# Attention over clusters with two MLPs on one core: a second product in unsplit float32, cluster dots in four column groups, and a new set of priorities

## The chip, the cores and the metric

The kernel runs on one core of one Trainium2 chip, as one program. The metric is the device time of one execution in microseconds; of several executions the median is given.

## The reference

For 2 batches of 8 heads, 768 tokens and a head width of 64, every query and key is assigned to one of 16 centroids of its head, and a query sees the keys of its own cluster only. The heads' outputs, put side by side as 1536 tokens of width 512, go through two MLPs.

```python
q_assign = np.argmax(np.einsum('bhsd,hcd->bhsc', q_n, c_n), axis=-1)
k_assign = np.argmax(np.einsum('bhsd,hcd->bhsc', k_n, c_n), axis=-1)
mask = q_assign[:, :, :, None] == k_assign[:, :, None, :]
scores = np.where(mask, scale * np.matmul(q, k.transpose(0, 1, 3, 2)), -1e9)
attn = softmax(scores); x = np.matmul(attn, v)
h = np.maximum(x @ w_in, 0.0)
y = h * h @ w_out
out = (1.0 / (1.0 + np.exp(-(y @ w_gate))) * (y @ w_val)) @ w_out2
```

Here `softmax` stands for the lines that subtract the maximum, exponentiate and divide by the sum. The weights of the MLPs come as 64-bit words and are turned into float32 on the chip.

## The kernel before, in words

**Attention.** There are 96 score tiles, 6 to each of 16 heads, of 128 queries by 768 keys. A tile `s` is made on TensorE (`t_qk`), its row maximum on VectorE (`t_max`, line 978), its exponential on ScalarE (`t_exp`, line 993). Then most tiles are split into two halves of 16 bits, the high one by ScalarE (line 330) and the low one by VectorE (`t_lo`, line 1018, which frees the score bank), transposed by a DMA, and multiplied with the values on TensorE (`po`). Twelve pairs of tiles (`by_pe`) stay in float32 and are transposed by TensorE instead (`t_turn_pe`, line 1055, tiles `tb` and `ptf`). A few tiles (`by_pool`) are split by GpSimd.

**Cluster assignment.** For every four heads the products of queries and keys with the centroids (`CB`) are made in two halves (`half_dots`, line 671) in a bank `ah`. Rows of tokens are the stationary operand there, so that tokens come out on partitions: twelve matmuls of 32 columns to a half. `half_most`, `half_reach` on VectorE, `half_turn` on TensorE, `half_keep`, `half_count` and `half_first` then find the first largest centroid. The first two heads are assigned ahead of all others by `pair_dots` (line 445) with the operands the other way round: four matmuls of 384 columns, each into 32 partitions of its own (tile `as`). Seven half-groups go by `half_dots`. The tiles `T` and `M` are the operands of the scores, built from the raw queries and keys and the assignment.

**MLPs.** Tokens are taken in three chunks of 512. Nearly every product is made of float32 operands cut into two parts that TensorE takes at full rate (type fp32r): high by high, high by low and low by high, so three matmuls. Weights are loaded as words, turned into float32 (`magnitude` to `lower`, tiles `wi0m`, `wo0m` and so on) and split by `split_tasks` (line 1391, `wo0h` and `wo0l`); the first MLP's hidden tiles are squared into the bank and split by `split_bank` (line 1423, `g_..h` and `g_..l`). Of the first MLP (`g1` and `g2`, products `g` and `y`) chunk 0 is worked off by itself, in four groups of four hidden tiles; its tokens are complete after the first batch. Chunks 1 and 2 follow, and then the second MLP (`pg`, `pv`, `o`).

**The order of the work.** A planner (class `Planner`) walks through time once, when the program is built. Each piece of work has the engines on which it can run with an estimated cost, a priority, the buffers that it takes and gives back, and sometimes a gate on how far ahead it may run. Of the pieces that are ready, an engine takes the one with the lowest priority number, and that fixes the order of every engine's instructions. The numbers of `PLAN` (line 32) set the priorities, the gates and what an engine's time is worth. Where the planner sees a hole on TensorE during attention, `fill` (line 617) puts matmuls there whose results are not used:

```python
n = min(8, int((gap - 700) // 250))
```

All plain matmuls stand on line 323, ScalarE's copies on line 330, VectorE's on 332 and GpSimd's on 334.

Of the kernel before, what the change touches and what calls it, by code (L numbers as in the profile page):

```python
# [32 lines left out]
    "asg_p": -2000, "assign": 15, "assign_step": 2.0, "base": 70, "build": 4, "build2": 6.4,  # L33
    "clamp_p": -1700, "conv": 8, "conv_gate": 14, "d": 3.8, "dup_a": 1700, "dup_p": 900,
    "dup_q": 200, "e_bufs": 2, "exp": 1.6, "g_gate": 3, "g_split": -7.9, "group": 4, "h_gate": 11,
    "h_split": 2.1, "hi": 3.9, "hi_a": -1000, "hi_p": 99999, "hip_p": 600, "hip_v": 400,
    "keep_x_v": 1700, "lead": 0, "lead2": 7, "lead_min": 10, "lead_slope": 0, "lo": -0.2,
    "lo_v": 600, "load_gate": 8, "margin": 5, "max": 1, "oh_p": 900, "pe_keep": -1.9,
    "pe_keep_v": 300, "pe_turn": 1.6, "pv": -1.7, "pv_pe": 5.1, "qk": 2.0, "qk_hi_a": -200,
    "qk_hi_p": 2500, "qk_lo_v": -100, "qk_sc_p": -400, "raw": 30, "relu": 1.7, "s_hi_a": -500,  # L40
    "s_hi_p": 1800, "s_lo_v": -1400, "spare": 0, "split_gate": 8, "square_v": 900, "third": 1,
    "turn": 13.3, "v_hi_a": 1200, "v_hi_p": 1300, "v_later": 100000, "v_lo_v": 700, "v_split": 19,
    "v_stat": 11, "w_hi_a": -900, "w_hi_p": -100, "w_lo_v": -800, "w_load": 8.2, "w_mag_v": 3100,
    "w_split": 3.0, "wait_a": 0.2, "wait_p": 1.0, "wait_q": 0, "wait_t": 0, "wait_v": 0,
    "worth_a": 600, "worth_p": 0, "worth_v": 1200, "x": -1.3, "x0": 109, "x1": 226, "x_gate": 5,
    "x_split": 3.4, "y_gate": 12, "y_keep": 7.1, "y_keep_v": 500, "y_split": -4.3,
    "by_pe": (1, 4, 7, 10, 13, 16, 19, 21, 23, 26, 30, 33,),
    "by_pool": (3, 14, 53, 71, 72,),
# [6 lines left out]
class Task:  # L55


    __slots__ = ("fn", "on", "prio", "waits", "users", "left", "ready", "take", "give", "gate", "end", "price", "port")

    def __init__(self, fn, on, prio, after, take, give, gate, kind, port):  # L60
        self.fn, self.on, self.prio = fn, on, prio

        self.port = port
# [21 lines left out]
class Planner:  # L85


    def __init__(self, start):
        self.free = dict(start)
        self.units = {}  # L90
        self.avail = []
        self.freeing = []
        self.count = 0
        self.total = 0
        self.port = 0.0
        self.fill = None

    def add(self, fn, on, prio, after=(), take=(), give=(), gate=None, at=0.0, kind="", port="vp"):
        t = Task(fn, on, prio, after, take, give, gate, kind, port)
        t.ready = max(t.ready, at)  # L100
        self.total += 1
        if not t.left:
            self.avail.append(t)
        return t

    def start(self, t, e, now):
        for res, n in t.take:
            self.units[res] -= n
        if e == "t" and self.fill is not None:
# [20 lines left out]

    def can(self, t, e, now):
# [6 lines left out]
        if t.gate is not None and not t.gate():  # L138
# [4 lines left out]
    def soon(self, best, e, now):  # L143
# [7 lines left out]
            and (u.gate is None or u.gate())  # L151
# [36 lines left out]
def kernel(  # L188
# [77 lines left out]
    def provide(name, pool, tag, n):  # L266
        places.setdefault(name, []).append([pool, tag, [0] * n])
        units[name] = units.get(name, 0) + n
# [1572 lines left out]
```

## Time and profile before

| what | value |
|---|---|
| median of 3 runs | 824.47 us (823.18 to 824.98) |
| span of the profiled execution | 821.0 us |
| busy: TensorE, VectorE, ScalarE, GpSimd | 783.9, 551.2, 456.1, 236.4 us |
| mean granted clock of TensorE | 0.977 |
| data moved by DMA | 96.85 MB |

The profile gives the span of one execution, from its first to its last instruction. Its own whole time is not recorded apart; the runs' times hold the span and what lies around it, and the median is 3.5 us above the span. In the rows PE is TensorE's matmuls, PEld its weight loads, DVE VectorE, ACT ScalarE, POOL GpSimd. PEclk is the clock that TensorE was granted as a share of full speed. An arrow with a name behind a row's idle time says which instruction ended the wait. A float32 matmul appears as two records.

### The profile page before, as it was taken

The numbers are of one execution on the slowest core, as the hardware profiler recorded it, in microseconds if no ns is written. First come the engines' busy times: TensorE is split into PE (matmuls) and PEld (weight loads), VectorE is DVE, ScalarE is ACT, GpSimd is POOL, SyncE is SP. The second block draws the span as 40 slices with busy tenths as digits, with TensorE's granted clock in tenths as the row PEclk, the third lists the DMA queues.
The fourth block names the chain that finished last, engine by engine and source line by source line (L and its number), as shares of the span: only waits on it lengthen the run. The fifth ranks groups of instructions, "written<-read, shape, count | busy, mean of one in ns | idle before, by whom it ended". The sixth has DMA issues, their size and how long they took to land.

```text
span 821.0 us, 12751 instructions
## 1 busy us (share of the span) xinstructions
PE 783.9 (95%) x4869; PEld 657.1 (80%) x4869; DVE 551.2 (67%) x885; ACT 456.1 (56%) x822; POOL 236.4 (29%) x304
## 2 busy tenths in 40 slices
PE   7898988999998989899999999999999999999998
PEld 4687978897887867688888888888888888888886
DVE  7889788879999997968375868844334437960300
ACT  8768779869887775578483654422222225630300
POOL 7755434845564222303030322200010004200000
PEclk9989899989999999999999999999999999999999
DMA  7777887758798998424131323312111213100101
GB/s 246 139 155 166 169 171 207 146 110 174 168 197 151 213 208 267 142 94 151 52 129 58 126 74 103 128 52 97 58 51 55 100 51 107 48 26 26 40 26 39
DMA packets 133742, 96.85 MB, mean 118 GB/s; under 512 B 114800, under 2 KB 114992, under 8 KB 133680
## 3 DMA queue, kind: packets, MB, share of 16 engines
q1 hardware_dynamic: 133680, 96.03, 46.1%
q8 instruction: 38, 0.62, 0.3%
q14 instruction: 24, 0.20, 0.1%
HBM read 62.10 MB, written 3.15 MB: 79 GB/s over the span
## 4 chain that ended last, share of the span: by engine, by line
PE 59%; ACT 0%; issue 0%
PE y L323 12%; PE o L323 12%; PE pv L323 12%; PE pg L323 12%; PE g L323 11%; PE xq L1245 0%; ACT ot L1631 0%
## 5 line engine op out<-in xcount | busy, mean ns | idle before, releaser
L323 PE MATMUL s<-M,T 128*128 128x384 f32 x360 | 87.9, 374 | 15.0 <-DVE hl L1018 10.5
L978 DVE TENSOR_REDUCE nm<-s 128x1 f32<-128x768 f32 x96 | 89.9, 949 | 12.4 <-PE s L323 12.0
L1602 DVE SCALAR_TENSOR_TENSOR gv<-th,pv 128x512 f32<-128x512 f32 x36 | 24.6, 687 | 87.7 <-PE pv L323 86.3
L323 PEld LDWEIGHTS s<-M,T 128*128 128x128 f32 x360 | 64.2, 202 | 23.2 <-DVE hl L1018 9.5
L1595 ACT ACTIVATE th<-pg 128x512 f32<-128x512 f32 x36 | 21.5, 598 | 109.9 <-PE pg L323 109.9
L993 ACT ACTIVATE s<-s,nm 128x768 f32<-128x768 f32 x70 | 61.2, 874 | 22.6 <-DVE nm L978 22.3
L1018 DVE TENSOR_TENSOR hl<-s,hl 128x768 f16<-128x768 f32 x70 | 65.9, 946 | 7.8 <-ACT hl L330 7.6
L330 ACT ACTIVATE hl<-s 128x768 f16<-128x768 f32 x70 | 56.4, 814 | 0.5
L1631 ACT ACTIVATE ot<-o 128x512 f32<-128x512 f32 x12 | 7.2, 598 | 79.4 <-PE o L323 79.4
L323 PEld LDWEIGHTS <-pt 128*128 128x128 f16 x1296 | 43.1, 101 | 9.1 <-issue 6.5
L1339 POOL TENSOR_SCALAR wgm<-wgm 128x512 f32<-128x512 f32 x12 | 8.6, 719 | 141.1 <-ACT wgm L1331 125.9
L323 PE MATMUL po<-vh,pt 128*128 128x64 f16 x864 | 47.0, 197 | 1.9 <-DMA pt<-hl 1.2
L323 PE MATMUL po<-vl,pt 128*128 128x64 f16 x432 | 44.2, 197 | 0.0
L323 PEld LDWEIGHTS po<-vr,ptf 128*128 128x128 f32 x288 | 38.2, 208 | 0.9 <-DVE xp L1110 0.8
L323 PE MATMUL po<-vr,ptf 128*128 128x64 f32 x288 | 37.9, 288 | 0.0
L1571 DVE TENSOR_TENSOR yf<-yf,y 128x512 f32<-128x512 f32 x36 | 24.6, 684 | 16.3 <-PE y L323 15.8
L1529 ACT ACTIVATE r<-g 128x512 f32<-128x512 f32 x48 | 28.7, 597 | 11.3 <-PE g L323 10.6
L1339 POOL TENSOR_SCALAR wi1m<-wi1m 128x512 f32<-128x512 f32 x16 | 10.1, 633 | 76.3 <-ACT wi1m L1331 64.9
L915 POOL TENSOR_TENSOR T<-raw,T 64x768 fp32r<-64x768 f32 x14 | 26.6, 1898 | 17.8 <-ACT T L330 9.1
L1535 ACT ACTIVATE g<-r 128x512 f32<-128x512 f32 x48 | 29.0, 604 | 1.1
L921 POOL TENSOR_TENSOR M<-raw,M 64x768 fp32r<-64x768 f32 x15 | 28.1, 1871 | 1.0
L993 ACT ACTIVATE e<-s,nm 128x768 f32<-128x768 f32 x26 | 23.5, 905 | 7.6 <-DVE nm L978 7.2
(605 smaller groups left out, 2390.8 us busy)
## 6 DMA issues: line engine op xcount, KB each, us to landing
wi0r<-in_moe_w_in_dram SPq DMA_DIRECT2D x16, 512.0 KB, 4.0
wo0r<-in_moe_w_out_dram SPq DMA_DIRECT2D x16, 512.0 KB, 4.7
wi1r<-in_moe_w_in_dram SPq DMA_DIRECT2D x16, 512.0 KB, 3.3
wo1r<-in_moe_w_out_dram SPq DMA_DIRECT2D x16, 512.0 KB, 3.3
wgr<-in_moe_w_gate_dram SPq DMA_DIRECT2D x12, 512.0 KB, 3.3
wvr<-in_moe_w_val_dram SPq DMA_DIRECT2D x12, 512.0 KB, 3.3
w2r<-in_moe_w_out_dram SPq DMA_DIRECT2D x12, 512.0 KB, 3.3
raw<-in_q_dram SPq DMA_DIRECT2D x8, 384.0 KB, 4.7
```

The lines of the kernel that those rows point to most:

```text
L323: nc.tensor.matmul(o, lhsT=l, rhs=r, start=a, stop=z)
L330: nc.scalar.activation(out=out, in_=in_, func=AF.Copy, scale=scale)
L915: eng(e).tensor_tensor(out=T1[j][q], in0=raw[k][r], in1=T1[j][r].bitcast(F32), op=ALU.subtract)
L921: eng(e).tensor_tensor(out=M2[j][r], in0=raw[k][r], in1=M1[j][r].bitcast(F32), op=ALU.subtract)
L978: nc.vector.tensor_reduce(out=NM[n], in_=sc_ps[n][:, :, :HS], axis=AX.XY, op=ALU.max, negate=True)
L993: nc.scalar.activation(out=y, in_=x, func=AF.Exp, bias=NM[n], accum_out=SM[n // NQ][:, i : i + 1],)
L1018: nc.vector.tensor_tensor(out=halves(hl[:, n % 2, 1]), in0=x[:, :, :HS], in1=halves(hl[:, n % 2, 0]), op=ALU.subtract,)
L1529: nc.scalar.activation(out=r, in_=banks["g1", c, f], func=AF.Relu)
L1535: nc.scalar.activation(out=p, in_=r, func=AF.Square)
L1571: nc.vector.tensor_tensor(out=yf[c, dm], in0=yf[c, dm], in1=p, op=ALU.add)
L1595: nc.scalar.activation(out=t, in_=p, func=AF.Tanh, scale=0.5)
L1602: nc.vector.scalar_tensor_tensor(out=o, in0=t, scalar=1.0, in1=p, op0=ALU.add, op1=ALU.mult)
```

## The change

It does three things. For 12 of the 16 hidden tiles of chunk 0 (groups 0, 1 and 3, named by `whole`) the second product of the first MLP takes the weights and the squared activations unsplit, in float32, one matmul in place of three. The dots of `half_dots` have their operands exchanged: four matmuls of 384 columns, each into 32 partitions; a copy (`half_out`) and three transposes (`half_flip`) then bring tokens onto partitions. And nearly all numbers of `PLAN` are others, `by_pe` and `by_pool` among them. Besides, the planner's estimates of these pieces are set to the new form, the score operands are given back by every tile of a head instead of the last, and gates and pools are counted where a piece is planned instead of by closures.

```diff
 PLAN = {
-    "asg_p": -2000, "assign": 15, "assign_step": 2.0, "base": 70, "build": 4, "build2": 6.4,
+    "asg_p": -3875, "assign": 14.0, "assign_step": -3.1, "base": 80, "build": 4.0, "build2": 6.3,
...
-    "by_pe": (1, 4, 7, 10, 13, 16, 19, 21, 23, 26, 30, 33,),
-    "by_pool": (3, 14, 53, 71, 72,),
+    "by_pe": (1, 4, 7, 10, 13, 16, 19, 23, 26, 33, 35, 45),
+    "by_pool": (41, 44, 56, 81, 86, 93),
+    "nudge": {},
+    "whole": (0, 1, 3),
...
+        for s in range(2):
+            for y in range(2):
+                pl, h0 = (y, hf) if gp > 0 else (-gp, y)
+                r0 = s * 64 + y * 32
+                mm(
+                    a[r0 : r0 + 32, :HS], CB[:, 2 * gr + pl].rearrange("p j c -> p (j c)"),
+                    raw[s, b, 2 * gr + pl][:, h0 * HS : (h0 + 1) * HS], True, True,
+                )
+        AX_[gp, hf] = a
+
+    def half_out(e, gp, hf):
+        if hf == 0:
+            AX_[gp, "d"] = at.tile([P, S], F32, tag="d", name=f"d{gp % (NG + 1)}")
+        copy(e, AX_[gp, "d"][:, hf * HS : (hf + 1) * HS], AX_[gp, hf][:, :HS])
+
+    def half_flip(gp, hf):
         for x in range(3):
-            for s in range(2):
-                for y in range(2):
-                    pl, t = (y, 3 * hf + x) if gp > 0 else (-gp, 3 * y + x)
-                    c0 = x * P + s * 64 + y * 32
-                    mm(
-                        a[:, c0 : c0 + 32], raw[s, b, 2 * gr + pl][:, t * P : (t + 1) * P],
-                        CB[:, 2 * gr + pl].rearrange("p j c -> p (j c)"), True, True,
-                    )
-        AX_[gp, hf] = a
+            nc.tensor.transpose(
+                AX_[gp, hf][:, x * P : (x + 1) * P],
+                AX_[gp, "d"][:, hf * HS + x * P : hf * HS + (x + 1) * P], ident,
+            )
...
-                dots, {"t": 2400}, pr, after=last + [x for k in keys for x in raw_after(*k)],
+                dots, {"t": 680}, pr, after=last + [x for k in keys for x in raw_after(*k)],
...
+            t = add(
+                lambda e, gp=gp, hf=hf: half_out(e, gp, hf), {"a": 400, "v": 465}, pr + st_,
+                kind="ptk", after=[t], port="",
+            )
+            t = add(lambda e, gp=gp, hf=hf: half_flip(gp, hf), {"t": 330}, pr + st_, after=[t])
...
+            if f in self.whole:
+                self.split[f, uses[0]] = [self.conv[f]]
+                return
...
+    WHOLE = [f for f in range(NF1) if f // gsize(0) in PLAN["whole"]]
+    W2 = [Weights(w_out, f"wo{c}", False, w2[c], () if c else WHOLE) for c in range(2)]
...
+        if c == 0 and f in WHOLE:
+            h = slab(F32, f"h{c}_{f}")
+            hT[c, f] = [h]
+            if e == "a":
+                nc.scalar.activation(out=h, in_=r, func=AF.Square)
+            else:
+                nc.vector.tensor_tensor(out=h, in0=r, in1=p, op=ALU.mult)
+            drop(p)
+            drop(r)
+            return
...
+        if c == 0 and f0 in WHOLE:
+            ops = [(W.m[f][:, ds_], hT[c, f][0]) for f in range(f0, f0 + gs)]
```

What it moves is seen in the order of the instructions. On PE, the dots of one half of heads 4 to 7 of the first batch (`ah` is their bank, `raw` the queries and keys, `eq` and `tw` the later steps, `po` the product with the values); first before, then with the change:

```order
L323 MATMUL ah_1_220_832<-CB,raw_0_2_12_137 128x32
L323 MATMUL ah_1_220_832<-CB,raw_0_3_50_313 128x32
L323 MATMUL ah_1_220_832<-CB,raw_0_2_13_139 128x32
L323 MATMUL ah_1_220_832<-CB,raw_0_3_56_322 128x32
...
L323 MATMUL ah_1_220_832<-ident_150,eq_1_888 128x128
...
L323 MATMUL ah_1_220_832<-tw_1_933,before 128x384
```

```order
L344 MATMUL ah_1_189_747<-raw_0_2_12_137,CB 32x384
L344 MATMUL ah_1_189_747<-raw_0_3_50_314,CB 32x384
L344 MATMUL ah_1_189_747<-raw_0_2_13_139,CB 32x384
L344 MATMUL ah_1_189_747<-raw_0_3_78_389,CB 32x384
L344 MATMUL po_184_734<-vr_0_4_121,ptf_160_641 128x64
...
L713 MATMUL ah_1_189_747<-ident,d_540 128x128 x3
L344 MATMUL s_198_776<-M_0_109,T_0_105 128x384 x2
```

Before, the first four rows come three times. Now they come once, and behind six matmuls of another tile follow the transposes, which read `d`, ScalarE's copy of the dots; the next score tile is queued behind them.

On PE, the first output tile `y` of group 0 of chunk 0 (`g_0h`, `g_0l` the split squares, `h_0` the unsplit one, `wo0h`, `wo0l`, `wo0m` the weights); before and with the change:

```order
L323 MATMUL y_0_0_878_2938<-g_0h_2641,wo0h_462_1653 128x512
L323 MATMUL y_0_0_878_2938<-g_0l_2648,wo0h_462_1653 128x512
L323 MATMUL y_0_0_878_2938<-g_0h_2641,wo0l_466_1664 128x512
L323 MATMUL y_0_0_878_2938<-g_1h_2730,wo0h_741_2548 128x512
L323 MATMUL y_0_0_878_2938<-g_1l_2741,wo0h_741_2548 128x512
L323 MATMUL y_0_0_878_2938<-g_1h_2730,wo0l_785_2668 128x512
```

```order
L344 MATMUL y_0_0_812_2754<-h_0_735_2479,wo0m_396_1410 128x512
L344 MATMUL y_0_0_812_2754<-h_1_768_2612,wo0m_600_2071 128x512
L344 MATMUL y_0_0_812_2754<-h_2_802_2709,wo0m_716_2407 128x512
L344 MATMUL y_0_0_812_2754<-h_3_805_2711,wo0m_775_2642 128x512
L344 MATMUL s_822_2773<-M_0_109,T_0_105 128x384 x2
```

Twelve matmuls to an output tile have become four, and a score tile stands right behind them.

On ACT, the hidden tiles 0 and 1 of chunk 0 (`r` the rectified tile, `ptf` and `hl` copies for attention, `e` and `s` exponentials, `sm` and `nm` their sums and maxima); before and with the change:

```order
L1529 ACTIVATE r_0_760_2589<-g_0_0_724_2469 128x512
L330 ACTIVATE ptf_758_2583<-tb_0_759_2584 128x512
L1535 ACTIVATE g_0_0_724_2469<-r_0_760_2589 128x512
L993 ACTIVATE e_770_2621,sm_746_2560<-s_755_2575,nm_763_2595 128x768
L1529 ACTIVATE r_1_778_2650<-g_0_1_744_2554 128x512
L330 ACTIVATE wo0h_779_2653<-wo0m_594_2059 128x512
...
L1535 ACTIVATE g_0_1_744_2554<-r_1_778_2650 128x512
L330 ACTIVATE wo0h_806_2721<-wo0m_787_2670 128x512
L330 ACTIVATE g_1h_2730<-g_0_1_744_2554 128x512
```

```order
L351 ACTIVATE d_2448<-ah_0_720_2419 128x384
L1565 ACTIVATE r_0_733_2456<-g_0_0_725_2428 128x512
L1574 ACTIVATE h_0_735_2479<-r_0_733_2456 128x512
L351 ACTIVATE T_1_106<-raw_1_1_299_1103 64x768
L351 ACTIVATE tw_0_2524<-ah_0_720_2419 128x384
L351 ACTIVATE M_1_110<-raw_1_1_358_1291 64x768
...
L1565 ACTIVATE r_1_763_2585<-g_0_1_743_2519 128x512
L1574 ACTIVATE h_1_768_2612<-r_1_763_2585 128x512
```

The squares go straight into `h`, the conversions to high parts (`wo0h`, `g_1h`) are gone from between them, and copies of `T`, `M` and `d` stand among them.

## Rows read from the trace of the kernel before

**Rows 1.** The page's summary of engines, and TensorE's clock in 40 slices.

```profile
PE 783.9 (95%) x4869; PEld 657.1 (80%) x4869; DVE 551.2 (67%) x885; ACT 456.1 (56%) x822; POOL 236.4 (29%) x304
...
PEclk9989899989999999999999999999999999999999
```

**Rows 2.** Windows by stage: length, busy time of each engine (instructions), clock, DMA share, GB/s.

```profile
0.00:24.00 24.00, 18.98 (x64) 11.63 (x65) 16.46 (x43) 18.10 (x33) 15.55 (x40) 0.93 0.69 223
24.00:138.00 114.00, 102.45 (x1084) 92.39 (x1083) 99.94 (x153) 91.06 (x177) 58.31 (x76) 0.94 0.79 170
138.00:301.00 163.00, 151.24 (x1376) 130.64 (x1375) 147.62 (x230) 133.37 (x241) 84.63 (x95) 0.95 0.84 168
301.00:337.00 36.00, 30.97 (x239) 25.22 (x238) 30.46 (x52) 22.21 (x42) 8.72 (x12) 0.97 0.82 241
337.00:821.00 484.00, 480.25 (x2112) 397.19 (x2110) 256.69 (x411) 191.38 (x333) 69.14 (x82) 1.00 0.22 74
```

**Rows 3.** The chain that ended last, in order of time: start us, us, what.

```profile
336.22 0.66 PE xq L1245 x4
336.87 12.54 PE y L323 x48
...
390.21 21.76 PE y L323 x96
...
719.33 97.93 PE o L323 x432
```

**Rows 4.** Waits of PE over the whole span: us in total, times, longest us.

```profile
PE s L323 <- DVE hl L1018: 11.1, 15, 2.2
...
PE s L323 <- ACT e L993: 2.4, 3, 1.1
...
PE ah L323 <- ACT tw L330: 1.2, 2, 0.6
```

**Rows 5.** PE's groups by form; its timeline from 6.2 us; line 323 from 6.9 us.

```profile
L1055 PE MATMUL tb<-ident,e 128*128 128x128 f32 x144 | 23.6, 288 | 4.2 <-ACT ptf L330 2.7 <-DVE ot L717 1.1 <-DVE sc L585 0.3
...
L323 PE MATMUL ah<-CB,raw 128*128 128x32 f32 x168 | 21.0, 285 | 0.0
...
L323 PE MATMUL fill<-ident 128*128 128x512 f16 x20 | 5.3, 380 | 0.5 <-DVE xp L1110 0.4
...
6.20 0.85 PE L323 MATMUL as<-raw,CB 128*32 128x384 f32 x8 [0.55 <-DVE CB L438]
...
L323 PE MATMUL busy<-raw,ident x14: 486/486/590, 7.0 to 11.3; 128*128 128x384 f32 x14
```

**Rows 6.** Windows around three dips of PE's clock; columns as in rows 2.

```profile
48.00:53.00 5.00, 5.00 (x44) 5.00 (x43) 4.92 (x8) 3.04 (x7) 2.12 (x3) 1.00 0.85 157
53.00:61.00 8.00, 7.46 (x49) 6.64 (x48) 6.38 (x9) 3.91 (x7) 3.56 (x5) 0.57 0.85 199
162.00:166.00 4.00, 3.38 (x32) 3.05 (x30) 2.87 (x5) 4.00 (x9) 3.76 (x4) 1.00 0.00 0
166.00:173.00 7.00, 7.00 (x32) 7.00 (x32) 4.31 (x7) 1.37 (x3) 2.03 (x3) 0.51 0.61 112
247.00:251.00 4.00, 2.33 (x10) 1.13 (x8) 4.00 (x8) 2.82 (x6) 0.12 (x1) 1.00 1.08 108
251.00:255.00 4.00, 3.38 (x40) 3.07 (x40) 4.00 (x7) 3.88 (x7) 0.51 (x1) 0.57 0.52 152
```

**Rows 7.** Groups by form on ACT and DVE: busy us, mean ns, idle before.

```profile
L330 ACT ACTIVATE T<-raw 64x768 fp32r<-64x768 f32 x13 | 10.9, 840 | 2.2 <-PE s L323 2.1
...
L330 ACT ACTIVATE wo0h<-wo0m 128x512 fp32r<-128x512 f32 x14 | 8.9, 632 | 1.6 <-DVE wo0m L1360 1.5
...
L1404 DVE TENSOR_TENSOR wo0l<-wo0m,wo0h 128x512 fp32r<-128x512 f32 x8 | 8.4, 1054 | 0.0
...
L1404 DVE TENSOR_TENSOR wi0l<-wi0m,wi0h 128x512 fp32r<-128x512 f32 x10 | 7.4, 737 | 1.0 <-ACT wi0h L330 0.7
...
L332 DVE TENSOR_SCALAR T<-T 64x768 fp32r<-64x768 f32 x7 | 5.2, 743 | 0.1
```

More of the change, by code (lines that the diff above doesn't have):

```diff
@@ L39 @@
[L39 to L44, printed above, removed]
@@ L55, with __init__ @@
 class Task:
-    __slots__ = ("fn", "on", "prio", "waits", "users", "left", "ready", "take", "give", "gate", "end", "price", "port")
-    def __init__(self, fn, on, prio, after, take, give, gate, kind, port):
+    __slots__ = ("fn", "on", "prio", "waits", "users", "left", "ready", "take", "give", "gate", "end", "price", "port", "place", "gain")
+    def __init__(self, fn, on, prio, after, take, give, gate, kind, port, place, gain):
         self.fn, self.on, self.prio = fn, on, prio
-        self.port = port
+        self.port, self.place, self.gain = port, place, gain
         self.price = {
@@ L95, in __init__, with add @@
         self.port = 0.0
+        self.place = 0
         self.fill = None
-    def add(self, fn, on, prio, after=(), take=(), give=(), gate=None, at=0.0, kind="", port="vp"):
-        t = Task(fn, on, prio, after, take, give, gate, kind, port)
+    def add(
+        self, fn, on, prio, after=(), take=(), give=(), gate=None, at=0.0, kind="", port="vp", place=None, gain=()
+    ):
+        prio += PLAN["nudge"].get(self.total, 0)
+        t = Task(fn, on, prio, after, take, give, gate, kind, port, place, gain)
         t.ready = max(t.ready, at)
@@ L108, in start @@
             self.units[res] -= n
+        for res, n in t.gain:
+            self.units[res] = self.units.get(res, 0) + n
+        if t.place is not None:
+            self.place = t.place
         if e == "t" and self.fill is not None:
@@ L129, in start, with open @@
                 self.avail.append(u)
+    def open(self, k, ahead, n):
+        if k > self.place + ahead:
+            return False
+        if not n:
+            return True
+        x = self.units["xn"]
+        return k <= self.place + 1 and x == 0 or self.units["S"] >= n + PLAN["spare"] + x
     def can(self, t, e, now):
@@ L137, in can @@
             return False
-        if t.gate is not None and not t.gate():
+        if t.gate is not None and not self.open(*t.gate):
             return False
@@ L150, in soon @@
             and all(self.units[r] >= n for r, n in u.take)
-            and (u.gate is None or u.gate())
+            and (u.gate is None or self.open(*u.gate))
             for u in self.avail
@@ L972, in t_qk @@
         sc_ps[n] = s
-        if n == NQ - 1:
+        if n < NQ and thold[0].readers == 0:
             drop(TM)
@@ L1290 @@
     at_ = {u: k for k, u in enumerate(order)}
-    pos = [0]
     BASE = PLAN["base"]
     def near(k, ahead):
-        return lambda: k <= pos[0] + ahead
-    def spare(k, n):
-        return k <= pos[0] + 1 and units["xn"] == 0 or units["S"] >= n + SPARE + units["xn"]
+        return (k, ahead, 0)
     def pr_of(k, early):
@@ L1372, in tasks @@
             )
-            def room():
-                return k <= pos[0] + CONVGATE and spare(k, 1)
+            room = (k, CONVGATE, 1)
             t = add(
@@ L1660 @@
                 t = add(
-                    started(k, lambda e, c=c, f=f, k=k, part=part: g1_part("g1", c, f, part, k)),
-                    {"t": 907}, pr, after=after, take=[("m", 1)] if part == 0 else [], give=give,
+                    lambda e, c=c, f=f, k=k, part=part: g1_part("g1", c, f, part, k),
+                    {"t": 907}, pr, place=k, after=after, take=[("m", 1)] if part == 0 else [], give=give,
                 )
@@ L1668 @@
             )
+            if c == 0 and f in WHOLE:
+                t = add(
+                    lambda e, c=c, f=f: square(e, c, f), {"a": 520, "v": 600}, pr - PLAN["h_split"], kind="square",
+                    after=[t], take=[("S", 1)], give=[hold("r", 1, 1), bh], port="",
+                )
+                hsplit[c, f] = [t]
+                continue
             t = add(
@@ L1689 @@
                 t = add(
-                    started(k, lambda e, c=c, g=g, dm=dm, part=part: g2_part(c, g, dm, part)),
-                    {"t": 113 * 3 * gs}, pr, after=after, take=[("m", 1)] if part == 0 else [],
+                    lambda e, c=c, g=g, dm=dm, part=part: g2_part(c, g, dm, part),
+                    {"t": 113 * 3 * gs if nx == 2 else 429 * gs}, pr, place=k, after=after, take=[("m", 1)] if part == 0 else [],
                     give=give if part else [],
@@ L1744 @@
                 t = add(
-                    started(k, lambda e, c=c, t=t_, part=part: g4_unit(e, c, t, part)),
-                    {"t": 2040}, pr, after=after,
+                    lambda e, c=c, t=t_, part=part: g4_unit(e, c, t, part),
+                    {"t": 2040}, pr, place=k, after=after,
                     take=[("m", 1)] if part == 0 else [],
```

87 lines of the change are left out of this document (47 added, 40 removed).

## The prediction

> **What bounds the kernel now.** I read the page's summary first: TensorE (PE) is busy for 783.9 of 821.0 us, 95%, and its clock row shows dips in the first 17 of 40 slices and almost none later [rows 1]. The windows by stage say where the other 37 us are [rows 2]. From 337 us on PE is busy for 480.25 of 484 us at full clock. The idle time lies ahead of that: 5.0 us in the start (0 to 24), 11.6 us in stage 1 (24 to 138, the score tiles of the first batch, with no other matmul work to fill in), 11.8 us in stage 2 (138 to 301, second batch, filled up with tokens 0 to 511 of the first MLP) and 5.0 us in stage 3 (301 to 337, what trails the last score tile). The chain that ended last confirms it: from 336.22 us it is PE alone, piece behind piece, to the end [rows 3]. So the whole time is PE's work plus the holes in the first 337 us. Cheaper work on another engine helps only where it closes a hole, and work added to PE costs its full length wherever it stands.
>
> The holes: PE's waits name VectorE (DVE) first, 11.1 us until the subtraction that frees a score bank; ScalarE (ACT) is behind 2.4 us of the same kind [rows 4]. DVE is busy for 147.62 of 163 us in stage 2, ACT for 133.37, PE for 151.24 [rows 2]: three engines near full, DVE with the least room to catch up. Besides holes there is a slower clock. The granted clock is 0.94 in stage 1 and 0.95 in stage 2 [rows 2], worth 6.8 and 8.2 us of work at full clock. It falls towards 1.2 GHz right behind the dots of 48 to 53 us, in which PE was busy the whole time with short matmuls, behind those of 162 to 166 us, and behind idle time as at 247 to 251 us [rows 6].
>
> **The change, part by part.** The profiled execution has a span of 821.0 us; the median of the runs is 824.47, 3.5 us more, which I add at the end.
>
> Dots. Seven half-groups of twelve 32-column matmuls take 21.0 us, 3.00 us each [rows 5]. Now each is four matmuls of 384 columns in four column groups, which the start of this kernel already does once: 0.85 us for the four, with the next matmul starting no later than they end. To this come three f32 transposes, 23.6 us / 144 = 0.164 us each, 0.49 us [rows 5]. 1.34 instead of 3.00 us, seven times: **-11.6 us** on PE. At the other end, four in a row at 0.66 us each (next paragraph but one) and 0.49 would be 3.14 us: +1.0 us in all. The row of the same shape decides for the first.
>
> The copy between dots and transposes is a new wait: the transpose stands on PE ahead of the next score tile, and the copy stands on ACT among exponentials. The nearest rows are PE's waits for an ACT copy of the same bank, 1.2 us in 2 of 7 cases, and for an exponential, at most 1.1 us [rows 4]. Bounds 0 and 7 x 1.1 = 7.7 us; I take the former's **+1.2 us**, since it is the same bank and engine.
>
> Second product. 48 f32 matmuls of 512 columns replace 144 at 21.76 / 96 = 0.227 us [rows 3]. The f32 price: `busy` is 7 matmuls of 384 columns, recorded as 14 halves that start from 7.0 to 11.3 us, so 0.662 us each, or 0.684 with the last one's 0.486 us counted in [rows 5]; for 512 columns 0.882 to 0.912. Against 3 x 0.227 = 0.680 this costs 48 x 0.202 = **+9.7 us**, at most +11.1. It is on PE, so nothing hides it.
>
> Fill matmuls fall from 20 to 14: 6 x 5.3 / 20 us [rows 5] = **-1.6 us**. PE's own sum is -11.6 + 1.2 + 9.7 - 1.6 = -2.3 us.
>
> The other engines. The unsplit product needs no high and low parts of 12 weight tiles and 12 activations. With the new priorities DVE loses 5 weight subtractions (1.054), 12 of activations (priced as the weight subtraction at 0.737) and 20 copies of T and M (0.743) [rows 7]: 29.0 us; in all, 63 fewer DVE instructions precede its last score maximum, 425 to 362, 15 of them in the first 48 tiles and 48 in the rest. ACT loses 21 high parts (0.632) but takes 12 copies of T and M (0.840) [rows 7] and the 7 new copies (under 0.632, being shorter): 346 to 351 instructions ahead of its last exponential. But they shift: 154 to 175 up to the 48th tile, 192 to 176 after it. None of this shortens the time by itself; it is worth what idle time it takes away.
>
> Stage 1: PE has four half-groups less to do (-6.6 us), but ACT has 21 more instructions. I let the stage shorten by half of PE's relief: **+3 us** idle. Bounds: -4 (a third of the 11.6 us goes) and +17.4 (rival 3). Stage 2: DVE's instructions there fall by a fifth (229 to 181) and ACT's by a twelfth, so of the 11.8 us I take half, **-6**; bounds 0 and -11.8. What is late next there is PE itself. Stage 3: 132 f32r matmuls and 16 f32 ones now stand behind the last score tile, where 144 f32r stood (44 instead of 33 us), so more work covers the trailing transfers: **-2**, bounds 0 and -5.0. They are work moved, not added.
>
> Clock: the spell behind the dots lost (1 - 0.57) x 8 = 3.4 us [rows 6]; that behind the dots of 162 to 166 us lost (1 - 0.51) x 7 = 3.4 us too. Full-width streaming in place of the short matmuls should spare one of the two: **-3.4**; bounds +3.4 (a new spell behind a hole in stage 1) and -10.
>
> Sum: -2.3 + 3 - 6 - 2 - 3.4 = -10.7; 821.0 - 10.7 = 810.3, and with 3.5 us **813.8 us**.
>
> **Rivals.**
> 1. Only PE's own sum counts; holes and clock stay: 821.0 - 2.3 + 3.5 = 822.2 us. For it: the chain from maximum to exponential to subtraction keeps its length per tile. Against: DVE stands behind the largest wait.
> 2. The relief is taken whole: half of stage 2's and 3's idle (-8.4), stage 1's unchanged, the clock's loss cut by three spells of 3.4 us (-10.2): 803.6 us. For it: the dips of the clock that the rows show come right behind dots or a hole [rows 6], so what closes holes also spares dips. Against: three engines are near full, so one lighter engine leaves two.
> 3. ACT sets the pace of stage 1. 21 instructions at 91.06 / 177 = 0.514 us [rows 2] are 10.8 us. If ACT's present idle time there (23 us, in which it waits for maxima) cannot take them, the stage is 10.8 us longer while PE has 6.6 us less to do: 17.4 us more idle instead of 3, 828.2 us. It decides from 13.7 us on; there the time is that of before. Against: the idle time is twice the added work. For: ACT also carries the new copy on which PE waits.
> 4. The change doesn't do what it says: the four matmuls follow one another. That is 12.6 us on the forecast, 826.4 us. The `as` rows speak against it: `as` starts at 6.20, lasts 0.85 and so ends at 7.05 us, and `busy` starts at 7.0 [rows 5]. The Trainium skill (TensorEngine Tiling (Array Packing), Key Properties) says that a change of tiling mode drains the engine. By that, two drains for each of seven half-groups, estimated from the page's rule at a record's tail of 0.155 us (0.486 less 0.331), would add 2.2 us: 816.0 us; the trace shows no such gap behind `as`.
>
> **How the numbers follow.** Forecast 0.47 (its own range 807 to 821), rival 1 0.20, rival 2 0.15, rival 3 0.13, rival 4 0.05. The range reaches from rival 2's lower part to most of rival 3: 802 to 827 us. A measurement of this kernel can tell about 0.2% from no change, so faster means under 822.8 and slower over 826.1: faster 0.45 + 0.15 + two thirds of rival 1 and a little of the others, 0.75; within 0.2% 0.10; slower 0.15.
>
> **What would show it.** Dots of about 0.85 us in four overlapping matmuls and `y<-h` at 0.88 us spacing; PE's wait for the subtraction well under 11.1 us; DVE about 30 us or more lighter ahead of the last score tile, and that tile well ahead of 300 us; a clock above 0.95 in stage 2; PE unbroken from the end of attention on. I am wrong if stage 1 is not shorter, with ACT as releaser of PE's waits, if the transposes wait for their copies by more than 3 us in sum, or if the f32 matmul comes out near 1.0 us.

## The result, and the profile after

The changed kernel takes 797.88 us (797.35 to 798.74, median of 4), where the kernel before took 823.83 us in runs beside it: a ratio of 0.9718, with a 95% interval of 0.9673 to 0.9762. The forecast was 813.8 us in a range of 802 to 827. The direction was right; the gain is about two and a half times the one forecast, and the time lies 4.1 us below the range.

The page's summary of the changed kernel's profiled execution, of 796.3 us, against [rows 1]:

```profile
PE 768.2 (96%) x4724; PEld 621.6 (78%) x4724; DVE 505.8 (64%) x822; ACT 460.3 (58%) x839; POOL 251.0 (32%) x308
...
PEclk9999999999999999999999999999999999999999
```

No slice of the clock row is below 9. VectorE (DVE) is busy for 45 us less, ScalarE (ACT) for 4 us more. The windows by stage follow, with the columns of [rows 2]; the borders are again the 48th score tile, the last one and the end of attention, which now come at 128, 272 and 311 us instead of 138, 301 and 337.

```profile
0.00:24.00 24.00, 19.14 (x74) 10.94 (x75) 17.49 (x44) 20.33 (x40) 15.16 (x44) 1.00 0.66 210
24.00:128.00 104.00, 91.85 (x974) 76.25 (x973) 86.41 (x136) 97.91 (x187) 65.24 (x77) 0.98 0.87 186
128.00:272.00 144.00, 136.69 (x1296) 108.11 (x1297) 118.82 (x183) 123.48 (x225) 75.75 (x86) 0.99 0.92 185
272.00:311.00 39.00, 39.00 (x289) 33.20 (x288) 37.26 (x62) 28.39 (x53) 16.05 (x19) 1.00 0.79 228
311.00:796.00 485.00, 481.51 (x2096) 393.09 (x2094) 245.86 (x402) 190.23 (x338) 78.81 (x85) 1.00 0.23 77
```

Stage 1 went from 114 to 104 us, stage 2 from 163 to 144; what trails the last score tile takes 39 instead of 36, with no idle time in it, and the rest is as long as before. The waits of TensorE (PE) over the whole span, to be held against [rows 4]:

```profile
PE s L344 <- DVE hl L1055: 4.8, 7, 1.6
PE po L344 <- DMA pt<-hl: 4.2, 6, 1.6
PE tb L1092 <- DVE ot L749: 3.6, 4, 1.1
PE ah L344 <- ACT tw L351: 1.4, 2, 1.0
...
PE s L344 <- ACT e L1030: 0.3, 1, 0.3
```

The wait for the subtraction that frees a score bank fell from 11.1 to 4.8 us, that for an exponential from 2.4 to 0.3.

Three sums tell where the 24.7 us between the two spans went. Idle time is the span less PE's busy time. Lost clock is the span times what the mean granted clock lacks of 1; it is an upper bound, since it counts idle time at the lower clock too. Work is what is left: PE's busy time at full clock.

| kernel | span | work | idle | lost clock (mean clock) |
|---|---|---|---|---|
| before | 821.0 | 765.0 | 37.1 | 18.9 (0.977) |
| changed | 796.3 | 764.2 | 28.1 | 4.0 (0.995) |
| difference | -24.7 | -0.8 | -9.0 | -14.9 |
| forecast of the difference | -10.7 | -2.3 | -5 | -3.4 |

The forecast of work has the 1.2 us in it that PE was to wait for copies. So PE does as much work as before; between these two executions the time came from lost clock first and from idle time second. In the forecast it was the other way round, and both were smaller. How the gain divides between the two depends on the execution that is taken: against e1 below, another execution of the kernel before, the three differences are -1.3, -11.1 and -4.1 us, with idle time first.

### The profile page after: what moved, and what is told of

It reads as the page before. It is cut to its first block, busy times and chain, and to the rows that moved or that the text cites. A ratio compares the mean times of both kernels' runs of the same rounds, so it can differ in the third digit from the quotient of the medians.

```text
span 796.3 us, 12473 instructions
## 1 busy us (share of the span) xinstructions
PE 768.2 (96%) x4724; PEld 621.6 (78%) x4724; DVE 505.8 (64%) x822; ACT 460.3 (58%) x839; POOL 251.0 (32%) x308
## 4 chain that ended last, share of the span: by engine, by line
PE 66%; ACT 1%; DVE 0%; issue 0%
PE y L344 14%; PE g L344 14%; PE o L344 12%; PE pv L344 12%; PE pg L344 12%; PE po L344 1%; PE s L344 0%; PE xq L1280 0%; ACT hl L351 0%; ACT s L1030 0%; PE tb L1092 0%; ACT wi0m L1362 0%; DVE hl L1055 0%; DVE nm L1015 0%; ACT e L1030 0%
## 5 line engine op out<-in xcount | busy, mean ns | idle before, releaser
L344 PE MATMUL s<-M,T 128*128 128x384 f32 x360 | 83.9, 363 | 4.1 <-DVE hl L1055 3.3
L1055 DVE TENSOR_TENSOR hl<-s,hl 128x768 f16<-128x768 f32 x66 | 62.1, 950 | 13.6 <-ACT hl L351 13.0
L1030 ACT ACTIVATE s<-s,nm 128x768 f32<-128x768 f32 x66 | 57.6, 872 | 10.9 <-DVE nm L1015 10.5
L351 ACT ACTIVATE hl<-s 128x768 f16<-128x768 f32 x66 | 52.5, 814 | 0.3
L1436 POOL TENSOR_TENSOR wgl<-wgm,wgh 128x512 fp32r<-128x512 f32 x10 | 14.3, 1428 | 95.5 <-ACT wgh L351 95.5
L344 PE MATMUL y<-h,wo0m 128*128 128x512 f32 x96 | 44.1, 597 | 0.0
L344 PEld LDWEIGHTS po<-vr,ptf 128*128 128x128 f32 x288 | 34.0, 192 | 4.5 <-DVE xp L1147 1.8
L1620 DVE TENSOR_TENSOR yf<-yf,y 128x512 f32<-128x512 f32 x36 | 24.6, 684 | 12.5 <-PE y L344 12.3
L1370 POOL TENSOR_SCALAR wi1m<-wi1m 128x512 f32<-128x512 f32 x16 | 16.3, 1019 | 49.0 <-ACT wi1m L1362 34.9
L1030 ACT ACTIVATE e<-s,nm 128x768 f32<-128x768 f32 x30 | 27.0, 902 | 6.9 <-DVE nm L1015 6.7
L344 PEld LDWEIGHTS y<-h,wo0m 128*128 128x128 f32 x96 | 17.5, 190 | 15.8 <-issue 14.8
```

The costliest lines, as they stand in the source:

```text
L344: nc.tensor.matmul(o, lhsT=l, rhs=r, start=a, stop=z)
L351: nc.scalar.activation(out=out, in_=in_, func=AF.Copy, scale=scale)
L1030: nc.scalar.activation(out=y, in_=x, func=AF.Exp, bias=NM[n], accum_out=SM[n // NQ][:, i : i + 1],)
L1055: nc.vector.tensor_tensor(out=halves(hl[:, n % 2, 1]), in0=x[:, :, :HS], in1=halves(hl[:, n % 2, 0]), op=ALU.subtract,)
L1370: eng(e).tensor_scalar(out=self.m[f], in0=self.m[f], scalar1=MOST, scalar2=LEAST, op0=ALU.min, op1=ALU.max,)
L1436: eng(e).tensor_tensor(out=l, in0=self.m[f], in1=h.bitcast(F32), op=ALU.subtract)
```

## The experiments

They try these theories. **A**: the narrow dots cost work and bring the clock down. **B**: holes bring the clock down, and a lighter VectorE and the new priorities close them. **P** and **O**: the gain lies in which engine does what (prices), or in the order and the gates. **F**: it lies in one order that is fitted to its pieces, so that any other order of the same pieces is longer. **H**: more fill in the holes would hold the clock up. The comparisons go against runs of the kernel before on the same chip, and times are medians. The sums are those of the profiled executions:

| kernel | time | span | work | idle | lost clock |
|---|---|---|---|---|---|
| e1, before again | 818.49 | 812.8 | 765.5 | 39.2 | 8.1 |
| e2, wide dots, old numbers | 820.0 | 818.4 | 758.2 | 47.9 | 12.3 |
| e3, unsplit product, old numbers | 820.32 | 815.7 | 771.9 | 31.6 | 12.2 |
| e4, both, old numbers | 815.94 | 815.8 | 771.3 | 38.0 | 6.5 |
| e5, changed without unsplit product | 830.62 | 828.9 | 761.5 | 50.0 | 17.4 |
| e6, changed with narrow dots, replanned | 831.24 | 826.7 | 776.4 | 31.3 | 19.0 |
| e7, changed with old prices | 823.12 | 820.0 | 769.4 | 38.3 | 12.3 |
| e8, changed with old order and gates | 833.08 | 832.7 | 762.6 | 47.6 | 22.5 |
| e9, changed, narrow dots in its own order | 816.84 | 818.1 | 773.9 | 26.2 | 18.0 |
| e10, before with more fill | 823.67 | 816.3 | 770.4 | 33.7 | 12.2 |
| e11, changed, one number | 810.77 | 809.4 | 765.7 | 36.4 | 7.3 |
| e12, changed, another number | 807.43 | 805.8 | 767.8 | 33.2 | 4.8 |
| e13, before, wide dots in its own order | 819.06 | 817.7 | 756.9 | 46.9 | 13.9 |
| e14, before, one number | 832.03 | 828.7 | 768.8 | 42.5 | 17.4 |
| e15, before, another number | 821.34 | 819.6 | 770.1 | 37.2 | 12.3 |
| e16, changed with more fill | 799.24 | 795.8 | 772.9 | 22.9 | 0.0 |

The fill matmuls, which differ from plan to plan, are in the work; each is about 0.27 us [rows 5].

### The clock of the kernel before

No edit.

> The kernel before, unchanged, for the clock of its other executions. If the lost clock (0.977 in the profiled execution, 18.8 us of work at full clock) sets the time, executions with a lower clock are longer, by about 8.2 us for each 0.01 of mean clock, and all lie near 0.975 to 0.985. If the clock is mere accompaniment, time and clock do not go together.

Ten executions took 814.51 to 823.41 us at mean clocks of 0.990 to 0.975, and the others lie between: a straight line through the ten has 5.2 us for each 0.01 of clock (correlation 0.89), and the runs of the kernel before beside the four rounds of experiments give 5.5 to 7.9. The ratio to the runs of before beside it is 0.9981 (0.9956 to 1.0006), as it should be. Between the two profiled executions (821.0 and 812.8 us) the lost clock differs by 10.8 us, work by 0.5 and idle time by 2.1 the other way. So the clock is a price and not mere accompaniment, at two thirds or more of the 8.2 us that it could cost at most, and the kernel before varies by it on its own. Work came out as 765.5 us against 765.0: for one kernel that sum repeats to about half a microsecond.

### Each part with the old numbers

e2 has only the new `half_dots`, `half_out` and `half_flip` with their planned costs, e3 only the unsplit product, e4 both; the numbers of `PLAN` are those of before.

```diff
 PLAN = {
...
     "by_pe": (1, 4, 7, 10, 13, 16, 19, 21, 23, 26, 30, 33,),
     "by_pool": (3, 14, 53, 71, 72,),
+    "nudge": {},
+    "whole": (),
 }
```

For e3 and e4 the last entry is `(0, 1, 3)`; e3 keeps the old `half_dots`.

> The order numbers and split products of before, the dots in four column groups with the copy and the transposes. Theory A (the narrow dots bring TensorE's clock down): their 11.6 us go and the clock rises above 0.99, so 824 - 11.6 - 10 = about 802 us. Theory B (holes bring the clock down, and it is the lighter VectorE and the new priorities that close them): the 11.6 us turn in part into holes, the clock stays below 0.985, 813 to 820 us.

> The order numbers and dots of before, the second product of groups 0, 1 and 3 of tokens 0 to 511 unsplit. TensorE gets 48 x (0.859 - 0.680) = 8.6 us more. Theory A: the clock stays near 0.977 and the holes of the second batch shrink by at most 10 us: 820 to 832 us. Theory B: VectorE's and ScalarE's relief closes holes and spares dips of the clock in the second batch: 808 to 818 us, clock above 0.985.

> Dots and unsplit product together, with the order numbers of before. If the priorities set anew matter little, this is the changed kernel's time within 4 us (798 to 802). Theory A: about e2's time + 0 to 5. Theory B: clearly less than either alone, and the rest to 798 is the priorities'; 803 to 812.

Ratios to before: 0.9998 (0.9969 to 1.0028), 1.003 (0.9995 to 1.0065) and 0.9939 (0.9911 to 0.9966). Neither part gains anything alone, and both together 4 to 5 us. In e2 PE's work falls by 7 us, with 9 fill matmuls more in it, and idle time rises by 9 to 11. Its waits on PE:

```profile
PE s L344 <- DVE hl L1055: 10.5, 15, 1.9
PE po L344 <- DVE xp L1147: 7.4, 3, 5.8
PE po L344 <- DMA pt<-hl: 4.7, 4, 2.4
```

The first wait is about what it was [rows 4], and behind it stand waits for a divided output and for transposing DMAs: PE is done sooner and waits for attention's chain on the other engines. That is theory B's half of the expectation. In e3 idle time falls by 6 to 8 us and pays for 6 to 7 us of work, and the clock stays where it was (median 0.981): its time lies in theory A's range and not in B's. The time of e4 lies in none of the ranges expected. The rest of the way to 798 us must be the numbers, or what they make of the parts.

### Each part taken out of the changed kernel

e5 takes the unsplit product out, e6 the wide dots; the planner makes a new order for each. e7 and e8 put back the old prices, or the old numbers for order and gates.

```diff
-    "whole": (0, 1, 3),
+    "whole": (),
```

> The changed kernel with the second product split everywhere again (whole empty); priorities and dots as changed. With the old priorities the unsplit product was worth 4 us (820.0 to 815.9). If it is worth the same here: about 802 us, and the priorities alone carry some 18 us. If the priorities pay only together with the lighter VectorE: 810 us or more.

> The changed kernel with the narrow dots of before (twelve matmuls of 32 columns, no copy, no transposes). Theory A (narrow dots bring the clock down, and cost 11.6 us of TensorE): clock back to 0.98 to 0.985, 806 to 815 us. Theory B: what TensorE loses on dots falls into holes as it did with the old priorities: 798 to 803 us, clock above 0.99.

> The changed kernel with the old numbers for what each engine's time is worth (the keys that end in _a, _p, _v, _q and the three worth_), order, gates and picks as changed. VectorE takes 17 copies of T and M again, ScalarE 26 instead of 36. Theory P (the gain is in who does the work: copies off VectorE): 810 to 820 us. Theory O (it is in the order and the gates): 797 to 804 us.

> The changed kernel with the old numbers for order and gates, the prices, picks, dots and unsplit product as changed. VectorE has none of the copies of T and M. Theory P: 797 to 804 us. Theory O: 810 to 820 us. If both this and the run with old prices lie between 802 and 812, the two only pay together.

Every one is as long as the kernel before or longer: ratios to before of 1.0088 (1.0057 to 1.0118), 1.0124 (1.0087 to 1.0162), 1.0012 (0.9979 to 1.0045) and 1.0116 (1.0025 to 1.0207). Neither P nor O alone holds the gain, and the 25 to 35 us between these runs and the changed kernel are far more than the 8 to 10 us of work that a part is to PE. The times of e6, e7 and e8 lie above every range expected of them; that of e5 fits the expectation that the priorities pay only with the lighter VectorE, but a plan that its pieces no longer fit would give the same. The windows of e5 for stage 2 and for all behind attention show where its time is, for instance:

```profile
129.50:279.60 150.10, 130.46 (x1297) 111.78 (x1298) 119.01 (x179) 127.37 (x233) 75.00 (x83) 0.93 0.84 167
...
313.10:828.90 515.80, 505.86 (x2207) 416.36 (x2205) 272.79 (x443) 205.79 (x366) 84.78 (x97) 0.99 0.24 79
```

Stage 2 has 20 us idle where the changed kernel has 7, at a clock of 0.93; behind attention, where more work is left, 9.9 us are idle instead of 3.5. What these four runs measure is likely in the main a plan that no longer fits, so they can't price a part. For that the order has to be held.

### The dots in a kept order

e9 issues the twelve narrow matmuls where the changed kernel has the four wide ones, with the order of every engine as it is; the transposes are left out, and ScalarE's copy is made but not used. PE's other matmuls come in the same sequence in both. e13 does the opposite in the kernel before: the wide matmuls, the copy on ScalarE and the transposes stand together where the narrow ones stood.

```diff
# e9
...
     def half_flip(gp, hf):
-        for x in range(3):
-            nc.tensor.transpose(
...
+        pass
# e13
         AX_[gp, hf] = a
+        half_out("a", gp, hf)
+        half_flip(gp, hf)
```

> The changed kernel with the order of every engine kept, and the twelve narrow matmuls issued where the four wide ones stood; the transposes are left out (they are not needed then), the copy on ScalarE is still made and not used. It tells the dots' own worth from that of the new plan. TensorE's work at full clock rises by about 9 us (8.7 to 8.9 between the replanned pairs). Theory A (narrow dots bring the clock down): besides, the clock falls from 0.996 to 0.985 or less: 812 us or more. Theory F (the loss of 33 us with replanned old dots was the unfitted plan): 803 to 809 us, clock above 0.99.

> The kernel before with the order of every engine kept, and the four wide matmuls, ScalarE's copy and the three transposes issued together where the twelve narrow matmuls stood. The counterpart to the narrow dots in the new order, which cost 19 us. Theory A (the narrow dots cost 9 us of work and bring the clock down): clock from 0.981 to 0.99 or more, time 804 to 813 us, less what TensorE waits for the copy (up to 1.5 us seven times). If the dots are worth little in the old order because its holes take what they free: 815 to 822 us with more idle time.

e9 takes 816.84 us, 19 us more than the changed kernel (ratio to before 0.9939, 0.991 to 0.9968). Of the 21.8 us between the two spans 9.7 are work and 14.0 lost clock, with idle time 1.9 us less. Windows of e9 around three of its half-groups of dots, columns as in [rows 2]:

```profile
36.00:41.00 5.00, 4.31 (x39) 4.04 (x37) 2.54 (x5) 3.81 (x9) 4.68 (x7) 1.00 0.88 164
41.00:48.00 7.00, 7.00 (x63) 6.69 (x63) 2.56 (x5) 3.87 (x7) 2.88 (x4) 0.55 0.50 94
55.00:58.00 3.00, 2.73 (x24) 2.60 (x23) 1.75 (x3) 2.98 (x6) 2.75 (x2) 1.00 1.07 199
58.00:65.00 7.00, 7.00 (x41) 6.69 (x41) 3.18 (x7) 2.60 (x6) 0.83 (x1) 0.55 0.24 70
111.50:113.00 1.50, 1.50 (x17) 1.50 (x15) 1.32 (x3) 1.48 (x3) 0.47 (x1) 1.00 0.59 83
113.00:120.00 7.00, 7.00 (x34) 7.00 (x34) 2.31 (x6) 3.64 (x8) 4.90 (x3) 0.53 1.09 210
```

Each first row of a pair holds dots at full clock, with PE busy for 86 to 100% of it; in the second the granted clock is 0.53 to 0.55, most of it at 1.2 GHz, although PE is busy to the full. The changed kernel, in the same order, has one short dip in its first 120 us, behind a hole (columns as in [rows 2]; PE is busy for 3.36 of the 5.00 us from 41 to 46, where the clock falls):

```profile
35.00:41.00 6.00, 6.00 (x82) 5.45 (x74) 2.95 (x6) 4.60 (x10) 5.67 (x6) 1.00 1.00 188
41.00:46.00 5.00, 3.36 (x45) 2.92 (x44) 3.78 (x7) 4.86 (x9) 1.65 (x5) 0.77 0.07 15
46.00:53.00 7.00, 7.00 (x54) 6.27 (x53) 4.65 (x7) 6.21 (x11) 4.47 (x3) 0.92 0.67 126
53.00:60.00 7.00, 5.87 (x66) 4.60 (x63) 6.83 (x12) 5.46 (x11) 3.34 (x3) 1.00 0.99 177
60.00:120.00 60.00, 53.64 (x615) 44.93 (x614) 50.85 (x79) 58.21 (x115) 34.56 (x38) 1.00 0.93 199
```

A hole of 0.69 us stands ahead of the same half-group in both kernels, so it isn't what sets them apart; here the clock falls behind the narrow dots and not behind the wide ones. First the changed kernel, then e9:

```profile
34.50 0.85 PE L344 MATMUL ah<-raw,CB 128*32 128x384 f32 x8 [0.69 <-ACT ptf L351]
```

```profile
37.38 2.87 PE L344 MATMUL ah<-CB,raw 128*128 128x32 f32 x24 [0.69 <-ACT ptf L351]
```

This shows theory A in the new order: about half of what the wide dots are worth there is the clock (14.0 of 21.8 us between the profiled executions; by the medians, 9.7 of the 19 us are work, which leaves some 9).

But not every half-group of narrow dots has a dip of the clock behind it, and most dips stand behind holes. In windows of half a microsecond e9 shows seven dips: four behind dots (12.0 us of lost clock) and three behind holes (5.1 us); behind the other three half-groups the clock stays. The profiled execution of the kernel before has eight. One is behind dots alone, at 53 us. The one at 166 us, which [rows 6] counts to the dots too, is less clear: a hole of 0.62 us ends at 163.66, and the dots begin at 165.10 us, 0.9 us before the clock falls. These two make 6.8 us. Six are behind holes (12.0 us), three of them here, each with what stands ahead of it:

```profile
81.00:84.00 3.00, 1.38 (x9) 0.93 (x7) 2.13 (x4) 3.00 (x7) 2.39 (x2) 1.00 1.39 217
84.00:91.50 7.50, 7.50 (x37) 7.40 (x36) 3.88 (x6) 3.90 (x9) 1.45 (x2) 0.54 0.81 214
196.50:200.00 3.50, 1.54 (x8) 1.02 (x7) 3.47 (x7) 3.47 (x8) 3.27 (x3) 1.00 0.70 127
200.00:204.00 4.00, 4.00 (x47) 3.76 (x46) 3.44 (x6) 2.96 (x6) 1.87 (x2) 0.57 0.94 174
297.00:299.00 2.00, 1.01 (x5) 0.74 (x5) 2.00 (x4) 1.97 (x4) 0.38 (x1) 1.00 1.28 231
299.00:303.00 4.00, 3.46 (x42) 2.99 (x41) 3.72 (x6) 2.53 (x5) 1.28 (x1) 0.57 0.83 200
```

The changed kernel has two left, both behind holes (3.4 us): the one above and this:

```profile
131.00:135.50 4.50, 1.41 (x43) 1.17 (x39) 1.32 (x4) 4.47 (x10) 4.17 (x9) 1.00 1.15 210
135.50:139.50 4.00, 3.61 (x12) 3.11 (x12) 3.07 (x6) 3.10 (x6) 3.66 (x5) 0.57 0.60 113
```

e1, the same kernel in another execution, has four, one of them behind dots. So holes bring the clock down too, as theory B has it, and in the kernel before they took most of what was lost.

In the old order the wide dots are worth little: e13 takes 819.06 us, a ratio of 0.9946 (0.992 to 0.9971), so 2 to 7 us. PE's work falls by 8.1 us, and idle time rises by 8 to 10 (against the two executions of before above). The clock has a median of 0.983, against 0.977 in the runs of before beside it, and the seven dips of its profiled execution all stand behind holes. Its windows of stages 1 to 3, and two waits of PE:

```profile
24.00:135.30 111.30, 93.44 (x1019) 78.02 (x1017) 100.66 (x153) 94.07 (x183) 57.50 (x77) 0.97 0.81 176
135.30:298.40 163.10, 146.76 (x1352) 123.31 (x1350) 148.03 (x230) 132.98 (x242) 83.29 (x95) 0.97 0.82 167
298.40:332.90 34.50, 30.55 (x237) 25.00 (x236) 30.79 (x52) 22.43 (x41) 9.27 (x12) 0.95 0.87 248
```

```profile
PE s L344 <- DVE hl L1052: 13.6, 16, 2.2
PE ah L715 <- ACT d L351: 4.3, 7, 0.6
```

In stage 1 PE is idle for 17.9 us where it was 11.6 [rows 2], while VectorE is busy for 100.66 of 111.3 us. 4.3 us of the new idle time are the copy, which ScalarE makes right behind the dots here; the wait for VectorE's subtraction is 13.6 us, about as in e1 (13.1). So the same edit gives back 19 us in one order and 2 to 7 in the other. What differs is what stands behind PE: VectorE is busy for 90% of stage 1 in e13 and for 83% in the changed kernel. That the lighter VectorE is what lets PE use the freed time is the likeliest reading of these rows; no run changed VectorE's load alone in a kept order.

### More fill

The planner's gap from which it fills is lowered, and up to 12 matmuls are put in; the order of all else is kept.

```diff
-        n = min(8, int((gap - 700) // 250))
+        n = min(12, int((gap - 300) // 230))
```

> The kernel before with 45 instead of 20 fill matmuls in the holes that the planner sees, the order of all else kept. Theory H (holes bring the clock down): the clock rises from 0.981 to 0.99 or more and the time falls by 3 to 7 us. Theory A (the narrow dots do): the clock stays below 0.985 and the time is the same or up to 3 us longer for the added work.

> The changed kernel with 41 instead of 14 fill matmuls in the holes that the planner sees, all else kept. Its clock leaves 2 to 3.4 us to win. If holes are what still brings the clock down: 795 to 797 us, clock 0.998 or more. If fill only adds work: 798 to 802 us.

Neither gains. The kernel before takes 823.67 us (ratio 0.9989, 0.9958 to 1.002) at a median clock of 0.979, no higher than without: theory H isn't borne out by the fill that the planner can place where the dots are narrow. It is no test of holes as such, for the 25 matmuls more leave 33.7 us idle where it was 37 to 39, and four of the five dips of the profiled execution still stand behind holes. The changed kernel reaches a clock of 1.0 in the profiled execution, but its work grows by 8.7 us for 5.2 us of idle time and 4.0 of clock: 799.24 us. There is nothing left to win that way, and this is no version better than the changed kernel.

### How much one number moves

```diff
# e11
-    "exp": 0.9
+    "exp": 1.0
# e12
-    "base": 80
+    "base": 81
# e14, in the kernel before
-    "assign": 15
+    "assign": 14.5
# e15, in the kernel before
-    "base": 70
+    "base": 71
```

> The changed kernel with one of its new numbers, the exponential's priority lead, 1.0 instead of 0.9. The planner then orders most of attention otherwise, with the same work (15 fill matmuls instead of 14). Theory F (the gain is that of one fitted order, and any other order of the same pieces is some 10 to 30 us longer): 808 us or more, clock below 0.99. Theory P or O (prices, gates and order rules carry it): 795 to 802 us.

> The changed kernel with the number that ranks the MLP's work against attention's 81 instead of 80; only the order from about the middle of the second batch on is another. Theory F: 803 us or more. Otherwise 796 to 801 us.

> The kernel before with one number another: the lead of the cluster assignment 14.5 instead of 15, which makes the planner order most of attention otherwise (35 fill matmuls instead of 20). If the old order was fitted to its pieces as the new one is (one number off there cost 9 and 13 us): 828 us or more. If not: 815 to 826 us.

> The kernel before with the number that ranks the MLP's work against attention's 71 instead of 70, as the changed kernel was run with 81 instead of 80 (9.5 us longer). If the old order was fitted too: 828 us or more. If not: 815 to 826 us.

One number costs the changed kernel 12.9 us (810.77; ratio to before 0.9857, 0.9838 to 0.9877) and 9.5 us (807.43; 0.9811, 0.979 to 0.983), of which 8.3 and 5.1 us are idle time, 1.5 and 3.6 work by the sums, with one fill matmul more. The clock of e11 is 0.991 to 0.996, not below 0.99 as theory F had it. Two of PE's waits in e11, the first of them for the subtraction:

```profile
PE s L344 <- DVE hl L1055: 9.3, 13, 1.6
PE po L344 <- DVE xp L1147: 4.0, 6, 0.9
```

9.3 us instead of 4.8. In the kernel before, one number cost 10 us (832.03; 1.0115, 1.0077 to 1.0153), with 15 fill matmuls more, some 4 us, among them; the other cost nothing (821.34; 0.9993, 0.9956 to 1.0031). So sensitivity to the order is no property of the new plan alone: with the same pieces one number moved the time by 0 to 13 us. Theory F holds so far that the new order is better than its two neighbours tried here; even those are some 7 to 11 us shorter, by the ratios, than e4, which has the same parts with the old numbers.

## Why the prediction was wrong, step by step

**What bounds the kernel**: right. The time is PE's work, its holes and its clock in the first 311 us; from then on PE works without a break, in pieces like those of [rows 3]:

```profile
310.92 13.74 PE y L344 x32
...
389.95 21.76 PE y L344 x96
...
694.59 97.93 PE o L344 x432
```

**Dots**: the four wide matmuls overlap as the start of the kernel showed. PE's timeline of the changed kernel, then that of e9 at the same place:

```profile
18.99 1.53 PE L344 MATMUL s<-TM 128*128 128x384 f32 x4 [1.48 <-DVE hl L1055]
20.45 0.85 PE L344 MATMUL ah<-raw,CB 128*32 128x384 f32 x8
21.23 1.56 PE L344 MATMUL s<-TM 128*128 128x384 f32 x4
22.73 0.55 PE L713 MATMUL ah<-ident,d 128*128 128x128 f32 x3
```

```profile
19.64 1.53 PE L344 MATMUL s<-TM 128*128 128x384 f32 x4 [1.04 <-DVE hl L1052]
21.00 2.76 PE L344 MATMUL ah<-CB,raw 128*128 128x32 f32 x24
```

The records of the four last 0.85 us, and the next matmul starts at 21.23, before they end at 21.30. By the starts there is a gap all the same. The next matmul starts 0.78 us behind the first of the four, where one such matmul takes 0.662 us [rows 5]; and the score matmuls ahead of the dots start 1.46 us before the wide ones, but 1.36 us before the narrow ones of e9. This 0.1 us at either end agrees with the rule of the Trainium skill (TensorEngine Tiling (Array Packing), Key Properties) that a change of tiling mode drains the engine. The prediction read no gap behind `as`, because it held a start against the end of a record; in seven half-groups it makes about 1.5 us. The work saved was sized at 11.6 us and measured 9.7 (e9) and 8.1 (e13). About 1.5 us of the 11.6 were lost clock and not work: one of the seven half-groups that make up 21.0 us ran at the lower clock and took 4.26 us, the others 2.76 to 2.85:

```profile
156.24 2.76 PE L323 MATMUL ah<-CB,raw 128*128 128x32 f32 x24
...
165.10 4.26 PE L323 MATMUL ah<-CB,raw 128*128 128x32 f32 x24
```

The **wait for the copy** was put at 1.2 us; PE's waits of the changed kernel do not name it, while with the copy right behind the dots it was 4.3 us in seven (e13), inside the bounds.

**Second product**: 32 records, so 16 float32 matmuls, in 13.74 us are 0.859 us each, where 0.882 was taken: 48 x (0.859 - 0.680) = 8.6 us instead of 9.7. PE's work in all: -0.8 against -2.3.

**Holes**: -9.0 us against -5, and -11.1 against the execution of e1. Stage 1 +0.6 (forecast +3), stage 2 -4.5 (-6), stage 3 -5.0 (-2): the relief behind the last score tile was put too low. Rival 3 did not come about: stage 1 is 10 us shorter, and PE's waits that ScalarE ends in it are 4.7 us, where they were 5.2. But ScalarE is now the fullest engine there, busy for 97.91 of 104 us; what it took on went into its idle time.

**Clock**: this is the step that failed. "Full-width streaming in place of the short matmuls should spare one of the two: -3.4" counted the two dips put down to dots in one execution, let one of them stay, and put nothing for the dips behind holes, though [rows 6] shows one at 251 us; its bound of -10 is less than the 15.0 us that the prediction itself read as lost in stages 1 and 2. In the profiled executions both of these two went (6.8 us), and of the six behind holes, 12.0 us, two with 3.4 us were left. So the clock gave back 14.9 us between the two profiled executions, and about 12.5 between the medians of the executions' clocks (0.981 for e1 and 0.9965 for the changed kernel, times some 810 us); at 5.2 to 8.2 us for each 0.01 that is worth 8 to 13 us. Against e1's execution it is 4.1 us only, so a part of the miss is chance: the sum started from an execution with much lost clock. Closing holes and sparing dips went together, as rival 2 had it: with -10.2 for the clock and -8.4 for holes, a chance of 0.15 and 803.6 us, it is the rival that came about, and it too fell short by the clock. The range ended just under it.

**The step under it**: the parts were priced one by one and added. They do not add. With the old numbers the dots alone are worth little or nothing (e2, e13), the unsplit product alone nothing (e3), both 4 to 5 us (e4); in the new order the dots alone are worth 19 us (e9). And the order itself was taken as neutral, where one number can move the time by some 10 us (e11, e12, e14). A range of 25 us around a sum of parts did not hold that.

**The span to the time**: 3.5 us were added, from a median of other executions than the profiled one; in the runs here the two are 1.7 us apart. That is 1.8 us of the error.

What stays open is how much of the remaining gain is the lighter VectorE and how much the order: each run that changed one changed the other. The unsplit product was not tried in a kept order, so what it is worth in the new one isn't known.

## What to carry to other kernels

When one engine is nearly full and the clock dips, add up work, holes and lost clock of that engine for both kernels before looking at single instructions: the sums show at once which of the three moved. Price a part by issuing it in an order that is held; taking it away and planning anew measures the plan. And look at the clock of several executions before a step is priced by one.

## What the runs showed of the hardware

A busy TensorE can lose its clock: behind float32 matmuls of 32 columns the granted clock fell to 0.53 to 0.57 over the next 7 to 8 us, at 53 us of the kernel before [rows 6], where PE was busy for 5.00 of 5.00 us ahead of it, and again, with the order of the changed kernel, in e9. It didn't fall each time: behind four of seven half-groups in e9, behind one in e1. Behind holes it fell with wide dots as well (both dips of the changed kernel, all seven of e13). Four float32 matmuls of 384 columns into four groups of 32 partitions made way for the next matmul 0.78 us behind the first start, where one by itself takes 0.66; a change between such groups and the whole array spread the starts by about 0.1 us. And a float32 matmul of 512 columns took 0.859 us, 3.8 times one of type fp32r (0.227).
